# Fused chunk attention and gated FFN on one core: another order of casts, turns and loads in the first two blocks, and block 3's DMA turns behind four stores

## The chip, the core and the metric

The kernel runs on one NeuronCore of a Trainium2 chip. The time is device microseconds of one execution. Of the kernel before, three timed runs are known, 254.26, 256.61 and 257.28 us (median 256.61), and one profiled execution of 255.33 us, from which all readings of the trace come.

## What is computed

Attention over 4 batches, 8 heads, 768 tokens of 64 channels, in chunks of 32 tokens; a chunk sees 8 memory rows, 16 tokens to the left, itself and 8 tokens to the right. The result, with heads side by side as 512 channels, goes through a gated FFN with 1536 hidden channels.

```python
for c in range(nc):
    q_c = q[:, :, c_start:c_end]
    k_full = np.concatenate([mem_k, k_ctx], axis=2)
    v_full = np.concatenate([mem_v, v_ctx], axis=2)
    scores = scale * np.matmul(q_c, k_full.transpose(0, 1, 3, 2))
    a = softmax(scores)
    out[:, :, c_start:c_end] = np.matmul(a, v_full)
x = out.transpose(0, 2, 1, 3).reshape(B * S, H * D)
return np.maximum(x @ w_gate, 0.0) * (x @ w_val) @ w_out
```

## The kernel before

**Blocks.** The 3072 tokens are cut into 8 blocks n of 384 (two for each batch). A block's attention goes by four head pairs hp, and inside a pair by four windows of 96 queries against 128 keys. The schedule is written out by hand: each engine does its instructions in the order of the code.

**Keys and queries transposed ("turned").** Blocks 0 and 1 turn on TensorE: `turn_pe` (L182) multiplies the rows by a selection matrix (`sel`, built on GpSimd by `build_sel`, L397) for the keys and by `ident` for the queries, and `turn_copy` (L207) evicts both with VectorE. Block 0 reads f32 rows over the SP and ACT queues (`kst`, `qst`) and casts them to `lk`, `lq` pair by pair (`cast_k`, `cast_q`, L158 and L162, on whatever engine is named); block 1 gets its rows cast by GpSimd's own DMAs (L478 to L481). From block 2 on, `turn_dma` (L214) issues two DMA transposes on the SP queue, one for `kT`, one for `qT`, and `spread_q` (L222) copies `qT` into the block-diagonal `qbd` with two GpSimd copies.

**Attention of a pair.** Scores on TensorE (`step_s0` L232 in blocks 0 and 1, which multiplies a mask in first; `step_s` L249 later) into the one PSUM tile `sc_ps`; the exponential on ScalarE; values (`wide_v` L293, `step_v` L268), whose sums of the softmax come out of the same product; then Ln and Exp on ScalarE give the reciprocal, and VectorE multiplies (`wide_m`, `step_m`) into `xT`.

**FFN.** `ffn_unit` (L341) makes 128 hidden channels of a block: 4 matmuls for the gate, 4 for the value, Relu on ScalarE, the product on VectorE. `out_unit` (L349) makes 128 tokens of output: 12 matmuls, a copy to `o_sb` on ScalarE, a store on the SP queue. The pool of `o_sb` has three buffers, the pool of PSUM tiles for turns, fillers, FFN and output (`fps`) four.

**The order around the change.** `fill(k)` issues k matmuls on zeros, which nothing reads. Block 0's turns, scores and values run first, then FFN unit 0 and 1 of block 0, block 1's turns, scores and values with its units 0 and 1, then units 2 to 11 of both blocks in turn (L563). After those come six output units u = 0 to 5 for blocks 0 and 1 (L578), with the attention of block 2 strewn between by the table `FIRST`; the scores of block 2's first pair stand ahead of u = 0. From block 2 on (L590) the attention of block n + 1 is strewn into the FFN of block n: the scores of block 3's first pair come after the 16 matmuls of block 2's FFN units 0 and 1.

GpSimd's queue carries: constants, block 0's values, a cast, the first 256 columns of both weights, two casts, block 1's rows and values, the other weight columns, `wo`, memsets, then for each block from 2 on `loads(n)` (4 DMAs of keys, 4 of queries, 4 of values) and `spread_q(n)`; `loads(n + 1)` stands behind `spread_q(n)`. A GpSimd DMA takes one of eight semaphores in turn, and waits until the DMA that had it last has landed. The SP queue carries the memory rows of a block (L139, L133), its two transposes and the stores. Before the change, block 3's transposes stand ahead of the stores of u = 0 to 5.

Of the kernel before, what the change touches and what calls it, by code (L numbers as in the profile page):

```python
# [18 lines left out]
def kernel(  # L19
# [31 lines left out]
    NFC = DM // 128  # L51
# [106 lines left out]
    def cast_k(hp, eng):  # L158
        eng(lk[:, hp].rearrange("p j h d -> p h j d"),
            kst[:, 2 * hp:2 * hp + 2, :].rearrange("p h (j d) -> p h j d", j=J))  # L160

    def cast_q(hp, eng):  # L162
        eng(lq[:, hp].rearrange("p j h d -> p h j d"),
            qst[:, 2 * hp:2 * hp + 2, :].rearrange("p h (j d) -> p h j d", j=J))
# [17 lines left out]
    def turn_pe(n, hp):  # L182

        kps = fps.tile([128, NQ, 128], F32, tag="f", name="k_ps")
        qps = fps.tile([128, 512], F32, tag="f", name="q_ps")[:, 0:TB]
        turns[n, hp] = kps, qps
        sel = sels[n].rearrange("p i t -> p (i t)")
        for j in range(J):
            kj = kps.rearrange("p i m -> p (i m)").rearrange("p (r j) -> p j r", j=J)[:, j]
            if n == 0:  # L190
                nc.tensor.matmul(kj, lhsT=lk[:, hp, j].rearrange("p h d -> p (h d)"), rhs=sel[0:KR + 2],  # L191
                                 start=True, stop=True)
            else:
                for hh in range(2):
                    nc.tensor.matmul(kj[D * hh:D * hh + D], lhsT=rk[:, 2 * hp + hh, j], rhs=sel[0:KR + 2],  # L195
                                     start=True, stop=True)
        for j in range(J):
            qj = qps.rearrange("p (r j) -> p j r", j=J)[:, j]
            if n == 0:
                nc.tensor.matmul(qj, lhsT=lq[:, hp, j].rearrange("p h d -> p (h d)"), rhs=ident[:QR, :QR],  # L200
                                 start=True, stop=True)
            else:
                for hh in range(2):
                    nc.tensor.matmul(qj[D * hh:D * hh + D], lhsT=rq[:, 2 * hp + hh, j], rhs=ident[:QR, :QR],
                                     start=True, stop=True)

    def turn_copy(n, hp):  # L207
        kps, qps = turns.pop((n, hp))
        if n not in qTs:
            qTs[n] = turned.tile([128, HP, TB], F16, tag="qT", name="qT0")  # L210
        dve_copy(kT_of(n)[:, :, hp, :], kps)
        dve_copy(qTs[n][:, hp, :], qps)
# [19 lines left out]
    def step_s0(n, hp):  # L232

        kT, qT = kT_of(n), qTs[n]
        sc = sps.tile([128, 2, 512], F32, name="sc_ps")
        mq = bass.AP(tensor=maskq.tensor, offset=maskq.offset, ap=[maskq.ap[0], [0, NQ], [1, QB]])
        for hh in range(2):
            nc.tensor.matmul(sc[:, hh, 0:TB].rearrange("p (i m) -> p i m", m=QB), lhsT=maskk, rhs=mq,  # L238
                             start=True, stop=False)
        for i in range(NQ):  # L240
            for hh in range(2):
                s = slice(D * hh, D * hh + D)
                nc.tensor.matmul(sc[:, hh, QB * i:QB * i + QB], lhsT=kT[s, i, hp, :],  # L243
                                 rhs=qT[s, hp, QB * i:QB * i + QB], start=False, stop=(i == NQ - 1))
        ex = epool.tile([128, 2, NQ, QB], F16, tag="ex", name="ex0")
        nc.scalar.activation(ex.rearrange("p h i m -> p h (i m)"), sc[:, :, 0:TB], ACT.Exp, scale=SCALE)  # L246
        exs[n, hp] = ex
# [45 lines left out]
    def wide_v(n, hp):  # L293

        ex = exs.pop((n, hp))
        vw = vwins[n % 2]
        if hp % 2 == 0:
            banks = [X[:, a, 0:TB] for a in range(2)]
        else:
            banks = [fps.tile([128, 512], F32, tag="f", name=nm)[:, 0:TB] for nm in ("xo_ps", "xs_ps")]  # L300
        for a in (1, 0):
            for i in range(NQ):
                for hh in range(2):
                    nc.tensor.matmul(banks[a][D * hh:D * hh + D, QB * i:QB * i + QB],
                                     lhsT=vw[:, i, 2 * hp + hh, D * a:D * a + D],
                                     rhs=ex[:, hh, i, :], start=True, stop=True)
        ln = rpool.tile([128, TB], F32, name="lnw")
        nc.scalar.activation(ln, banks[1], ACT.Ln, scale=1.0 / 64.0)
        rinv = rpool.tile([128, TB], F32, name="rinvw")
        nc.scalar.activation(rinv, ln, ACT.Exp, scale=-1.0, bias=mln64)  # L310
        wides[n, hp] = banks[0], rinv

    def wide_m(n, hp):
        o, rinv = wides.pop((n, hp))
        nc.vector.tensor_tensor(out=x_of(n)[:, hp, :], in0=o, in1=rinv, op=ALU.mult)  # L315
# [12 lines left out]
    def ffn_mm(n, order):  # L328
        for f, x in order:
            ps, w, m = units[n][x]  # L330
            nc.tensor.matmul(ps, lhsT=w[:, f, 128 * m:128 * m + 128], rhs=xTs[n][:, f, :],  # L331
                             start=(f == 0), stop=(f == NFC - 1))
# [57 lines left out]
    def mem_rows(p):  # L390
        src = bass.AP(tensor=mem16.tensor, offset=mem16.offset, ap=[mem16.ap[0], [0, NQ], [D, H], [1, D]])
        dve_copy(vwins[p][0:NMEM, :, :, 0:D], src)

    dve_copy(mem16, mem32)
    mem_rows(0)

    def build_sel(p):  # L397

        s = sels[p]
        nc.gpsimd.memset(s, 0.0)  # L400
        first = -6 if p == 0 else 10
        parts = [(0, NQ, 2, 32)] if p == 0 else [(0, NQ, 2, 30), (0, NQ - 1, 30, 32)]
        for i0, i1, t0, t1 in parts:
            ap = s[:, i0:i1, t0:t1]
            nc.gpsimd.affine_select(out=ap, in_=ap, compare_op=ALU.not_equal, fill=1.0,
                                    base=-first - t0, pattern=[[-24, i1 - i0], [-1, t1 - t0]], channel_multiplier=1)
        ap = s[:, :, 0:2]
        nc.gpsimd.affine_select(out=ap, in_=ap, compare_op=ALU.not_equal, fill=1.0,
                                base=-KR, pattern=[[0, NQ], [-1, 2]], channel_multiplier=1)
# [21 lines left out]
    def fill(count, cols=512):  # L431
        ps = fps.tile([128, 512], F32, tag="f", name="idle")
        for i in range(count):
            nc.tensor.matmul(ps[:, 0:cols], lhsT=filler[:, 0:128], rhs=filler[:, 0:cols], start=True, stop=True)  # L434

    act_copy = nc.scalar.copy
    fill(10)
    cast_k(0, dve_copy)
    cast_q(0, act_copy)
    turn_pe(0, 0)  # L440
    turn_copy(0, 0)
    fill(2)
    cast_k(1, act_copy)
    cast_q(1, act_copy)
    turn_pe(0, 1)
    fill(2)
    step_s0(0, 0)
    turn_copy(0, 1)
    cast_k(2, dve_copy)
    cast_q(2, pool_copy)  # L450
    load_w(wg, moe_w_gate, 0, 256)
    load_w(wv, moe_w_val, 0, 256)
    cast_k(3, pool_copy)
    cast_q(3, pool_copy)
    fill(2)
    step_s0(0, 1)
    turn_pe(0, 2)
    fill(1)
    wide_v(0, 0)
    turn_copy(0, 2)  # L460
    wide_v(0, 1)
    wide_m(0, 0)
    fill(2)
    turn_pe(0, 3)
    fill(1)
    step_s0(0, 2)
    turn_copy(0, 3)
    wide_m(0, 1)
    mem_rows(1)
    fill(2)  # L470
    step_s0(0, 3)
    wide_v(0, 2)
    wide_m(0, 2)
    fill(2)


    flat = rk.rearrange("p h j d -> p h (j d)")
# [1 line left out]
    for h0 in (0, 4):  # L479
        pool_dma(flat[0:KR, h0:h0 + 4], k_rows(1, h0, 4))  # L480
        pool_dma(rq.rearrange("p h j d -> p h (j d)")[:, h0:h0 + 4], q_rows(1, h0, 4))  # L481
    build_sel(1)
    load_band(1, v, vwins)
    for c0, c1 in ((256, 768), (768, 1280), (1280, 1536)):
        load_w(wg, moe_w_gate, c0, c1)
# [5 lines left out]
    for a in range(0, NDC, 4):  # L491
        pool_dma(wo[:, a:a + 4, :], wo_src[:, a:a + 4, :])

    wide_v(0, 3)
    wide_m(0, 3)
    ffn_open(0, (0,))
    for f in range(3):
        ffn_mm(0, [(f, 0), (f, 1)])
    turn_pe(1, 0)
    ffn_mm(0, [(3, 0), (3, 1)])  # L500
    ffn_close(0)
    turn_copy(1, 0)
    ffn_unit(0, 1)
    turn_pe(1, 1)
    step_s0(1, 0)
    turn_copy(1, 1)
    fill(2)
    step_s0(1, 1)
    turn_pe(1, 2)
    fill(1)  # L510
    wide_v(1, 0)
    turn_copy(1, 2)
    wide_v(1, 1)
    wide_m(1, 0)
    fill(2)
    turn_pe(1, 3)
    fill(1)
    step_s0(1, 2)
    turn_copy(1, 3)
    wide_m(1, 1)  # L520
    fill(2)
    step_s0(1, 3)
    wide_v(1, 2)
    wide_m(1, 2)
    fill(2)
    wide_v(1, 3)
    wide_m(1, 3)
    ffn_open(1, (0,))
    for f in range(4):
        ffn_mm(1, [(f, 0), (f, 1)])  # L530
    ffn_close(1)
    ffn_unit(1, 1)
# [24 lines left out]
    turn_dma(2)  # L557
    spread_q(2, pool_copy)
    loads(3)
    turn_dma(3)  # L560
    spread_q(3, pool_copy)

    for m in range(2, NDC):  # L563
        ffn_unit(0, m)
# [5 lines left out]
    def pieces(n, what):  # L570
        for w, hp in what:
            STEP[w](n, hp)
# [5 lines left out]
    for u in range(6):  # L578
        pieces(2, FIRST.get(2 * u, ()))
        out_unit(u // 3, u % 3, lambda: pieces(2, FIRST.get(2 * u + 1, ())))  # L580

# [58 lines left out]
```

## Time and profile before

| | |
|---|---|
| timed runs | 254.26, 256.61, 257.28 us, median 256.61 |
| the profiled execution | 255.33 us, of which the span of its instructions is 253.6 us |
| TensorE busy with matmuls | 235.2 us, 93% of the span |
| ScalarE, GpSimd, VectorE busy | 141.0, 113.2 and 99.1 us |
| moved by DMA | 28.95 MB, 114 GB/s on average |
| granted TensorE clock, mean | 0.980 |

The busy times are averages over stages of different kinds: a start, in which rows come in and the first two blocks are turned and scored (to 39.5 us), FFN units alone (39.5 to 66.8 us), output units with block 2's attention (66.8 to 94.7 us), and six blocks of FFN with the next block's attention between (from 94.7 us). What an edit is worth is read in its own stage, and in what stands behind it.

### The profile page before, as it was taken

The numbers are of one execution on the slowest core, as the hardware profiler recorded it, in microseconds if no ns is written. First come the engines' busy times: TensorE is split into PE (matmuls) and PEld (weight loads), VectorE is DVE, ScalarE is ACT, GpSimd is POOL, SyncE is SP. The second block draws the span as 40 slices with busy tenths as digits, with TensorE's granted clock in tenths as the row PEclk, the third lists the DMA queues.
The fourth block names the chain that finished last, engine by engine and source line by source line (L and its number), as shares of the span: only waits on it lengthen the run. The fifth ranks groups of instructions, "written<-read, shape, count | busy, mean of one in ns | idle before, by whom it ended". The sixth has DMA issues, their size and how long they took to land.

```text
span 253.6 us, 4446 instructions
## 1 busy us (share of the span) xinstructions
PE 235.2 (93%) x1682; PEld 135.8 (54%) x1682; DVE 99.1 (39%) x181; ACT 141.0 (56%) x268; POOL 113.2 (45%) x143
## 2 busy tenths in 40 slices
PE   6798998999999088999999999999999999999993
PEld 2554545666554045664666456655665566546641
DVE  6653644444311021662156314640565055604410
ACT  2165374333483455984588448955796378723311
POOL 8999479921990595079208920892040000000000
PEclk9799999999999859999999999999999999999999
DMA  7999999999599899919971997199620300020012
GB/s 180 199 146 168 206 194 206 160 151 101 35 144 140 208 118 172 129 36 155 192 134 20 135 200 139 26 130 207 114 41 4 124 1 3 0 105 19 3 41 83
DMA packets 114111, 28.95 MB, mean 114 GB/s; under 512 B 101834, under 2 KB 111018, under 8 KB 114090
## 3 DMA queue, kind: packets, MB, share of 16 engines
q0 software_dynamic: 84896, 14.74, 72.7%
q1 hardware_dynamic: 28362, 13.14, 24.6%
q10 hardware_dynamic: 832, 0.79, 1.2%
q8 instruction: 13, 0.21, 0.3%
q14 instruction: 8, 0.07, 0.1%
HBM read 31.16 MB, written 6.29 MB: 148 GB/s over the span
## 4 chain that ended last, share of the span: by engine, by line
PE 85%; ACT 5%; DMA 4%; issue 2%; DVE 1%; SPq 1%; ACTq 0%
PE v_ps L331 24%; PE g_ps L331 24%; PE o_ps L354 23%; PE x_ps L273 3%; PE sc_ps L253 3%; DMA out_dram<-o_sb 3%; DMA mem<-in_mem_v_dram 2%; PE idle L434 1%; PE sc_ps L238 1%; ACT ex L246 1%; PE k_ps L191 1%; PE sc_ps L243 1%; PE k_ps L195 1%; ACT ex L260 1%; ACT ln L276 1%
## 5 line engine op out<-in xcount | busy, mean ns | idle before, releaser
L339 DVE TENSOR_TENSOR gv<-v_ps,gr 128x384 f16<-128x384 f32 x96 | 53.5, 558 | 99.3 <-ACT gr L338 73.5
L331 PE MATMUL g_ps<-xT,wg 128*128 128x384 f16 x384 | 80.1, 326 | 1.6 <-DVE xT L315 1.2
L331 PE MATMUL v_ps<-xT,wv 128*128 128x384 f16 x384 | 80.0, 326 | 0.2 <-ACT o_sb L357 0.2
L354 PE MATMUL o_ps<-wo,gv 128*128 128x512 f16 x288 | 66.2, 387 | 0.0
L338 ACT ACTIVATE gr<-g_ps 128x384 f16<-128x384 f32 x96 | 46.7, 487 | 31.5 <-DVE gv L339 21.8
L331 PEld LDWEIGHTS <-wg 128*128 128x128 f16 x384 | 37.2, 98 | 23.9 <-issue 1.1
L331 PEld LDWEIGHTS <-wv 128*128 128x128 f16 x384 | 36.4, 98 | 23.8 <-issue 1.8
L226 POOL COPY qbd<-qT 64x1536 f16<-64x1536 f16 x12 | 17.5, 1462 | 68.1 <-DMA qT<-q16n 67.7
L354 PEld LDWEIGHTS <-gv 128*128 128x128 f16 x288 | 28.5, 100 | 33.1 <-issue 2.5
L357 ACT COPY o_sb<-o_ps 128x512 f32<-128x512 f32 x24 | 14.1, 587 | 44.0 <-PE o_ps L354 36.3
L288 DVE TENSOR_TENSOR xT<-x_ps,rinv 64x384 f16<-64x384 f32 x48 | 26.4, 550 | 26.8 <-ACT rinv L281 26.5
L260 ACT ACTIVATE ex<-sc_ps,bias 128x256 f16<-128x256 f32 x72 | 28.6, 467 | 2.6 <-PE sc_ps L253 2.5
L128 POOL DMA_DIRECT2D vwin<-in_v_dram x32 | 29.5, 948 | 0.6 <-issue 0.4
L276 ACT ACTIVATE ln<-x_ps 64x768 f32<-64x768 f32 x24 | 19.4, 807 | 13.8 <-PE x_ps L273 13.7
L281 ACT ACTIVATE rinv<-ln,mln 64x768 f32<-64x768 f32 x24 | 22.2, 924 | 0.1
L128 POOL DMA_DIRECT2D k<-in_k_dram x24 | 21.5, 905 | 0.0
L273 PE MATMUL x_ps<-ex,vwin 128*128 128x96 f16 x192 | 12.5, 209 | 8.0 <-ACT ex L260 8.0
L149 POOL DMA_DIRECT2D q16n<-in_q_dram x24 | 18.6, 801 | 0.0
L273 PEld LDWEIGHTS <-vwin 128*128 128x128 f16 x192 | 11.1, 99 | 11.9 <-DVE xT L288 7.8
L434 PE MATMUL idle<-filler 128*128 128x512 f16 x34 | 12.7, 478 | 1.3 <-DVE filler L370 1.3
L246 ACT ACTIVATE ex<-sc_ps 128x768 f16<-128x768 f32 x8 | 6.5, 811 | 9.9 <-PE sc_ps L243 9.9
L253 PE MATMUL sc_ps<-qbd,kT 128*128 128x192 f16 x96 | 11.8, 246 | 0.0
(70 smaller groups left out, 107.5 us busy)
## 6 DMA issues: line engine op xcount, KB each, us to landing
out_dram<-o_sb SPq DMA_DIRECT2D x24, 256.0 KB
vwin<-in_v_dram POOLq DMA_DIRECT2D x24, 120.0 KB, 5.7
q16n<-in_q_dram POOLq DMA_DIRECT2D x24, 96.0 KB, 4.4
k<-in_k_dram POOLq DMA_DIRECT2D x18, 120.0 KB, 4.4
wo<-in_moe_w_out_dram POOLq DMA_DIRECT2D x3, 512.0 KB, 13.4
wg<-in_moe_w_gate_dram POOLq DMA_DIRECT2D x2, 512.0 KB, 8.9
wv<-in_moe_w_val_dram POOLq DMA_DIRECT2D x2, 512.0 KB, 10.7
kst<-in_k_dram SPq DMA_DIRECT2D x4, 224.0 KB
```

The source lines that it names most:

```text
L128: pool_dma(dsts[p][NMEM + m0:NMEM + m1, i, :, 0:D], src)
L149: pool_dma(q16s[n][:, i], src)
L253: nc.tensor.matmul(sc[:, i // 2, 192 * (i % 2):192 * (i % 2) + 192], lhsT=kT[:, i, hp, :], rhs=qb[:, i, hp].rearrange("p h m -> p (h m)"), ...
L260: nc.scalar.activation(dst, src, ACT.Exp, scale=SCALE, bias=bias[:, g:g + 1])
L273: nc.tensor.matmul(X[:, hh, QB * i:QB * i + QB], lhsT=vw[:, i, 2 * hp + hh, :], rhs=ex[:, i, hh, :], start=True, stop=True)
L276: nc.scalar.activation(ln, X[D:128, :, 0:TB], ACT.Ln, scale=1.0 / 64.0)
L281: nc.scalar.activation(rinv, lns.pop((n, hp)), ACT.Exp, scale=-1.0, bias=mln64[0:D, :])
L288: nc.vector.tensor_tensor(out=xT[D * hh:D * hh + D, hp, :], in0=X[0:D, hh, 0:TB], in1=rinv[:, hh, :], op=ALU.mult)
L331: nc.tensor.matmul(ps, lhsT=w[:, f, 128 * m:128 * m + 128], rhs=xTs[n][:, f, :], start=(f == 0), stop=(f == NFC - 1))
L338: nc.scalar.activation(gr, g_ps, ACT.Relu)
L339: nc.vector.tensor_tensor(out=gvs[n][:, m, :], in0=v_ps, in1=gr, op=ALU.mult)
L354: nc.tensor.matmul(o_ps, lhsT=gvs[n][:, m, 128 * t:128 * t + 128], rhs=wo[:, m, :], start=(m == 0), stop=(m == NDC - 1))
```

## The change

It does four things.

**Block 0.** The first `fill` has 16 matmuls where there were 10. The memory rows for the values (a cast and a copy on VectorE) move from ahead of the first key cast to behind the first pair's eviction. Pair 0 is scored before pair 1 is turned; pairs 2 and 3 are turned before the scores of pairs 1 and 2. The key cast of pair 2 goes from VectorE to ScalarE, and GpSimd does its three casts before its first two weight loads, with block 1's `sel` built ahead of the casts. In all, fillers after the first batch go from 14 to 10.

**Block 1.** Unit 0 of block 0's FFN is no longer split around `turn_pe(1, 0)`, and the turns stand further ahead of the scores; fillers go from 10 to 2.

**Block 3.** `turn_dma(3)` and `spread_q(3)` move from ahead of the FFN units into the loop of output units, behind u = 3.

```diff
-    dve_copy(mem16, mem32)
-    mem_rows(0)
...
-    fill(10)
+    fill(16)
     cast_k(0, dve_copy)
     cast_q(0, act_copy)
     turn_pe(0, 0)
     turn_copy(0, 0)
-    fill(2)
+    fill(3)
     cast_k(1, act_copy)
     cast_q(1, act_copy)
+    build_sel(1)
+    dve_copy(mem16, mem32)
+    mem_rows(0)
+    step_s0(0, 0)
     turn_pe(0, 1)
+    turn_copy(0, 1)
+    cast_k(2, act_copy)
+    cast_q(2, pool_copy)
+    cast_k(3, pool_copy)
+    cast_q(3, pool_copy)
+    fill(3)
+    step_s0(0, 1)
+    turn_pe(0, 2)
+    turn_copy(0, 2)
     fill(2)
-    step_s0(0, 0)
-    turn_copy(0, 1)
-    cast_k(2, dve_copy)
-    cast_q(2, pool_copy)
+    wide_v(0, 0)
+    turn_pe(0, 3)
+    step_s0(0, 2)
+    turn_copy(0, 3)
+    wide_m(0, 0)
+    mem_rows(1)
+    wide_v(0, 1)
+    fill(1)
+    step_s0(0, 3)
+    wide_m(0, 1)
+    fill(1)
+    wide_v(0, 2)
+    wide_m(0, 2)
+    wide_v(0, 3)
+    wide_m(0, 3)
     load_w(wg, moe_w_gate, 0, 256)
     load_w(wv, moe_w_val, 0, 256)
-    cast_k(3, pool_copy)
-    cast_q(3, pool_copy)
-    fill(2)
-    step_s0(0, 1)
-    turn_pe(0, 2)
-    fill(1)
-    wide_v(0, 0)
-    turn_copy(0, 2)
-    wide_v(0, 1)
-    wide_m(0, 0)
-    fill(2)
-    turn_pe(0, 3)
-    fill(1)
-    step_s0(0, 2)
-    turn_copy(0, 3)
-    wide_m(0, 1)
-    mem_rows(1)
-    fill(2)
-    step_s0(0, 3)
-    wide_v(0, 2)
-    wide_m(0, 2)
-    fill(2)
...
-    build_sel(1)
     load_band(1, v, vwins)
...
-    wide_v(0, 3)
-    wide_m(0, 3)
     ffn_open(0, (0,))
-    for f in range(3):
+    for f in range(NFC):
         ffn_mm(0, [(f, 0), (f, 1)])
     turn_pe(1, 0)
-    ffn_mm(0, [(3, 0), (3, 1)])
+    turn_copy(1, 0)
     ffn_close(0)
-    turn_copy(1, 0)
     ffn_unit(0, 1)
     turn_pe(1, 1)
+    turn_copy(1, 1)
     step_s0(1, 0)
-    turn_copy(1, 1)
-    fill(2)
+    turn_pe(1, 2)
+    turn_copy(1, 2)
     step_s0(1, 1)
-    turn_pe(1, 2)
-    fill(1)
     wide_v(1, 0)
-    turn_copy(1, 2)
-    wide_v(1, 1)
-    wide_m(1, 0)
-    fill(2)
     turn_pe(1, 3)
-    fill(1)
     step_s0(1, 2)
     turn_copy(1, 3)
+    wide_m(1, 0)
+    wide_v(1, 1)
+    fill(1)
+    step_s0(1, 3)
     wide_m(1, 1)
-    fill(2)
-    step_s0(1, 3)
+    fill(1)
     wide_v(1, 2)
     wide_m(1, 2)
-    fill(2)
     wide_v(1, 3)
     wide_m(1, 3)
...
     loads(3)
-    turn_dma(3)
-    spread_q(3, pool_copy)
...
     for u in range(6):
         pieces(2, FIRST.get(2 * u, ()))
         out_unit(u // 3, u % 3, lambda: pieces(2, FIRST.get(2 * u + 1, ())))
+        if u == 3:
+            turn_dma(3)
+            spread_q(3, pool_copy)
```

**On the SP queue**, between block 3's memory rows and block 4's (`k_101` is block 3's key tile, `L359` a store of an output unit), the difference is this piece:

```order
 L133 DMA vwin_103<-mem 8x8x64 x4
+L359 DMA out_dram<-o_sb 128x512 x4
 L216 DMA_TRANSPOSE kT<-k_101 128x16x128
 L219 DMA_TRANSPOSE qT<-q16n 128x16x96
-L359 DMA out_dram<-o_sb 128x512 x6
+L359 DMA out_dram<-o_sb 128x512 x2
 L139 DMA k_100<-mem 8x4x512
```

The stores of u = 0 to 3 now stand ahead of block 3's two transposes, those of u = 4 and 5 still behind them. On GpSimd nothing moves there: `spread_q(3)` still stands between `loads(3)` and `loads(4)`.

**On GpSimd**, from the last constant to the first rows of block 1 (`lq_117` and `lk_116` are block 0's cast rows, `lk_118` and `lq_119` those of block 1, `sel_95` block 1's selection matrix), before:

```order
L427 AFFINE_SELECT maskq<-maskq 128x96
L163 CAST lq_117<-qst 96x2x4x64
L152 DMA wg<-in_moe_w_gate_dram 128x4x256
L152 DMA wv<-in_moe_w_val_dram 128x4x256
L159 CAST lk_116<-kst 114x2x4x64
L163 CAST lq_117<-qst 96x2x4x64
L478 DMA lk_118<-in_mem_k_dram 2x8x256
L480 DMA lk_118<-in_k_dram 112x4x256
```

and in the changed kernel:

```order
L424 AFFINE_SELECT maskq<-maskq 128x96
L397 MEMSET sel_95 128x128
L402 AFFINE_SELECT sel_95<-sel_95 128x4x28
L402 AFFINE_SELECT sel_95<-sel_95 128x3x2
L405 AFFINE_SELECT sel_95<-sel_95 128x4x2
L163 CAST lq_117<-qst 96x2x4x64
L159 CAST lk_116<-kst 114x2x4x64
L163 CAST lq_117<-qst 96x2x4x64
L152 DMA wg<-in_moe_w_gate_dram 128x4x256
L152 DMA wv<-in_moe_w_val_dram 128x4x256
L477 DMA lk_118<-in_mem_k_dram 2x8x256
L479 DMA lk_118<-in_k_dram 112x4x256
```

The two weight loads fall behind the other two casts and the building of `sel_95`, and every DMA behind them on this queue keeps its place in the row.

**On VectorE**, at the first cast (`mem_105`, `mem_106` are the memory rows in f32 and f16, `vwin_102` block 0's values), the changed kernel has:

```order
L379 MEMSET vwin_103 24x8x32
L159 CAST lk_116<-kst 114x2x4x64
L211 CAST kT<-k_ps 128x4x128
L212 CAST qT_196<-q_ps 128x384
L443 CAST mem_106<-mem_105 8x512
L392 COPY vwin_102<-mem_106 8x32x64
```

Before, the two operations on the memory rows stood between the memset and the key cast.

More of the change, by code (lines that the diff above doesn't have):

```diff
@@ L528 @@
     ffn_open(1, (0,))
-    for f in range(4):
+    for f in range(NFC):
         ffn_mm(1, [(f, 0), (f, 1)])
```

## Prediction

> **What bounds the kernel now.** I read the slices of the page first, then the busy time by stages, then the timeline of the stages in which TensorE isn't full.
>
> ```profile
> PE   6798998999999088999999999999999999999993
> PEclk9799999999999859999999999999999999999999
> 66.80:82.30 15.50, 15.47 (x102) 8.12 (x99) 2.76 (x5) 8.71 (x17) 8.98 (x11) 1.00 1.79 129
> 82.30:89.60 7.30, 0.00 (x0) 0.06 (x1) 1.10 (x2) 3.56 (x7) 4.24 (x4) 0.84 0.80 184
> 89.60:94.70 5.10, 5.07 (x20) 2.25 (x21) 1.10 (x2) 2.19 (x3) 5.10 (x7) 0.56 1.51 135
> 100.00:122.20 22.20, 22.20 (x152) 12.97 (x150) 9.98 (x18) 15.12 (x29) 12.97 (x14) 1.00 1.26 112
> ```
>
> TensorE is full and at full clock from 100 us to the last output unit, so the end comes as much earlier as block 3's first scores (97.66 us) do. Two places ahead of them aren't full: the start, and 82.3 to 89.6 us, an empty stretch with 5 us at 0.56 of the clock behind it. The second has its cause in these rows, of SP, GpSimd, ScalarE and TensorE:
>
> ```profile
> 72.35 3.66 SPq L216 DMA_TRANSPOSE kT<-k  x1
> 76.24 2.75 SPq L219 DMA_TRANSPOSE qT<-q16n  x1
> 79.09 16.77 SPq L359 DMA_DIRECT2D out_dram<-o_sb  x6
> 85.31 2.98 POOL L226 COPY qbd<-qT 64x1536 f16<-64x1536 f16 x2 [9.53 <-DMA qT<-q16n]
> 85.96 0.59 ACT L357 COPY o_sb<-o_ps 128x512 f32<-128x512 f32 x1 [7.63 <-DMA out_dram<-o_sb]
> 89.63 0.80 PE L273 MATMUL x_ps<-ex,vwin 128*128 128x96 f16 x8 [7.35 <-ACT ex L260]
> 90.22 4.66 PE L354 MATMUL o_ps<-wo,gv 128*128 128x512 f16 x12
> 67.15 2.75 PE L354 MATMUL o_ps<-wo,gv 128*128 128x512 f16 x12
> 97.66 0.49 PE L253 MATMUL sc_ps<-qbd,kT 128*128 128x192 f16 x4
> ```
>
> SP stands in its transposes while the first copies wait to be stored; with three `o_sb` buffers full, u = 3's copy waits 7.63 us for a store to land, ScalarE's queue stands behind it, and TensorE waits 7.35 us for an exponential. Its next 12 matmuls take 4.66 us where the same 12 took 2.75: 1.9 us more.
>
> **The stores ahead of the transposes.** First without any other shift. Unit 3 runs here:
>
> ```profile
> 76.26 2.75 PE L354 MATMUL o_ps<-wo,gv 128*128 128x512 f16 x12
> 94.72 0.33 PE L331 MATMUL g_ps<-xT,wg 128*128 128x384 f16 x1
> ```
>
> It ends at 79.0. Its copy no longer waits: it starts at 79.05 instead of 85.96. From that copy's start to the values of pair 3 the trace has 89.63 - 85.96 = 3.67 us (copy, Ln, Exp, exponentials), so these values come at 82.7, 0.6 us after TensorE has done unit 4. Then 8 matmuls (0.34), unit 5 (2.6 at full clock), and 97.66 - 94.72 = 2.94 us to the end of the 16 FFN matmuls: TensorE reaches block 3's first scores at 88.6 and not 97.66, **9.1 us earlier**. That removes the wait and its half clock.
>
> What is late next are the transposes, which began at 72.35 and now begin behind the fourth store: copy done at 79.65, store issued by 80.1. From the start of a turn to the first `qbd` copy the six turns differ:
>
> ```profile
> 50.90 4.26 SPq L216 DMA_TRANSPOSE kT<-k  x1
> 62.72 2.98 POOL L226 COPY qbd<-qT 64x1536 f16<-64x1536 f16 x2 [10.35 <-DMA qT<-q16n]
> 100.71 2.83 SPq L216 DMA_TRANSPOSE kT<-k  x1
> 109.17 2.98 POOL L226 COPY qbd<-qT 64x1536 f16<-64x1536 f16 x2 [10.60 <-DMA qT<-q16n]
> 127.93 2.01 SPq L216 DMA_TRANSPOSE kT<-k  x1
> 134.30 2.98 POOL L226 COPY qbd<-qT 64x1536 f16<-64x1536 f16 x2 [12.04 <-DMA qT<-q16n]
> 72.22 3.56 POOL L128 DMA_DIRECT2D vwin<-in_v_dram  x4
> 94.89 3.68 POOL L128 DMA_DIRECT2D vwin<-in_v_dram  x4
> 118.66 3.60 POOL L128 DMA_DIRECT2D vwin<-in_v_dram  x4
> ```
>
> 11.8 us for block 2, 13.0 for block 3 (72.35 to 85.31), 8.5 for block 4, 6.4 for block 5. Block 3's starts with the issue of its value loads, block 4's 2.1 us after the end of that issue (98.57), block 5's 5.7 us after it (122.26). In the new place block 3's value loads are all issued by 75.8, or 77.3 with the delay of the next part, and the turn starts 4 to 5 us later, so I take 6.4 and add 0.4 for the store just ahead on the same queue: 6.8; bounds 6.4 and 13.0. With the 2.98 us of the copies, `qbd` is ready 9.8 us after the turn starts: at 89.9, **1.3 us after TensorE gets there**.
>
> The page "DMA: Bandwidth & Descriptors" of the Trainium skill (Queues, rings and completion order) states that each DMA engine round-robins between its queues packet by packet; the four durations agree with that.
>
> **GpSimd's casts ahead of its weight loads.** These are the rows at that place, and the one at which the weight queue lets GpSimd go:
>
> ```profile
> 9.42 0.79 POOL L152 DMA_DIRECT2D wg<-in_moe_w_gate_dram  x1
> 10.20 0.76 POOL L152 DMA_DIRECT2D wv<-in_moe_w_val_dram  x1
> 11.29 0.86 POOL L159 CAST lk<-kst 114x512 f16<-114x512 f32 x1 [0.32 <-DMA kst<-in_k_dram]
> 12.65 0.60 POOL L478 DMA_DIRECT2D lk<-in_mem_k_dram  x1
> 16.96 3.96 POOL L128 DMA_DIRECT2D vwin<-in_v_dram  x4
> 33.41 0.74 POOL L492 DMA_DIRECT2D wo<-in_moe_w_out_dram  x1 [1.28 <-DMA wg<-in_moe_w_gate_dram]
> 66.82 0.49 PE L253 MATMUL sc_ps<-qbd,kT 128*128 128x192 f16 x4
> ```
>
> The key cast waits for rows until 11.29 in any order, so the casts end at 12.65 as before, and the weight loads are issued then, 3.2 us later than 9.42. Behind them block 1's rows are issued 0.79 + 0.76 = 1.55 us later; block 1's values, with `sel_95` already built, 0.65 us later. The DMA engines are the bound of this stream, for GpSimd waits at 33.41 for a weight load to land. So the whole stream is late by something between 0.65 (what the issues lose at last) and 3.2 (if no idle time of the engines makes up for any); I take **1.5**, the shift of block 1's rows. It passes on undiminished: the last `wo` load, the memsets, the loads of block 2, its turn at 50.90, and its `qbd`, ready at 62.72 + 2.98 = 65.70 before, at 67.2 now.
>
> **The start of blocks 0 and 1 gets shorter, for nothing.**
>
> ```profile
> 7.69 0.61 PE L191 MATMUL k_ps<-sel,lk 114*128 114x128 f16 x4 [2.10 <-DVE lk L159]
> 8.70:12.20 3.50, 3.50 (x16) 2.04 (x16) 2.33 (x5) 0.06 (x1) 3.18 (x6) 0.51 1.73 196
> 1.27 4.32 PE L434 MATMUL idle<-filler 128*128 128x512 f16 x10 [1.27 <-DVE filler L370]
> 6.62 0.68 DVE L392 COPY vwin<-mem 8x2048 f16<-8x2048 f16 x1
> 39.20 0.32 PE L331 MATMUL g_ps<-xT,wg 128*128 128x384 f16 x1 [0.54 <-DVE xT L315]
> ```
>
> Without the memory rows ahead of it the key cast can start about 1 us earlier, and 16 fillers end near 6.9 (ten in 4.32 us, six at the 0.22 us of 2.6 / 12); the first turn moves from 7.69 to about 6.9: 0.8 us. The 2.1 us gap goes, and with it the stretch at half clock that follows it (3.5 us at 0.51 in the row above, so 3.4 us at half): 1.7 us. Eight fillers fewer in block 1: 1.7 us. Sum 4.2, so the last of unit 0's inputs, 39.20 now, comes near 35; a wait for block 1's later rows is in this only as its lower bound, 0. If the new order of turns hides more, it is 5.5. TensorE would be through with the FFN units, which run without a gap, at 66.82 - 4.2 = 62.6.
>
> There it meets block 2's first scores, which stand ahead of unit 0 on TensorE and need the `qbd` of 67.2. It was 1.1 us from waiting there (65.70 against 66.82); it now waits **4.6 us**, and starts 0.4 us later than before. Whatever the start saves above nothing is lost here; this holds for any saving from 0 to 5.5.
>
> **The clock after that wait.** The 7.35 us gap cost 1.9 us of half clock, the 2.10 us gap 3.4 us of it. I take 1.9 for 4.6 us; bounds 0 (no drop) and 2.2 (0.56 on average over 5.1 us is 4.5 us at half clock, and half of that is lost).
>
> The page "TensorE: Matmul & The Clock Gate" of the Trainium skill (Part 1, What's actually happening) puts the drop at an idle window of about 3.4 us; by it the 4.6 us would do it, and half a window is an estimate of 1.7 us. The 2.10 us gap, shorter than such a window, dropped the clock too: the trace is stricter.
>
> **Sum.** Block 2's scores 0.4 later, half clock 1.9: everything behind shifts by 2.3. TensorE reaches block 3's scores at 88.6 + 2.3 = 90.9; the turn starts at 82.4 and `qbd` is ready at 82.4 + 9.8 = 92.2. So 92.2 against 97.66: **5.5 us gained**. The loads of block 4, behind `spread_q(3)`, start at 92.2 instead of 88.3. From the end of block 2's copies (65.70) to that of block 3's (88.29), at the slowest turn, went 22.6 us, so block 4's `qbd` is ready by 114.8; its scores come 25.7 us after block 3's,
>
> ```profile
> 123.33 0.49 PE L253 MATMUL sc_ps<-qbd,kT 128*128 128x192 f16 x4
> ```
>
> at 117.9. That cover, 3 us, holds. The profiled execution would take 255.33 - 5.5 = 249.8. The mean of the four known executions is 255.87, so I add 0.5: **250.3 us**.
>
> **Rivals.**
> 1. *The first wait costs no clock* (its gap falls across the windows in which the clock is set, or the start saves little). Then block 3's scores come at 80.1 + 0.4 + 9.8 = 90.3, 7.4 gained: 248.4. For it: of the 7.3 us from 82.3 some 5 passed at full clock (a mean of 0.84 is 2.3 us at half). Against it: both gaps seen dropped the clock in the end. With the stream late by only 0.65 it is 247.4.
> 2. *A turn like block 4's* (8.5 us), with a second drop of the clock after a wait of 3 us: scores at 82.4 + 8.5 + 3.0 = 93.9, and 1.8 of half clock: 2.0 gained, 253.8, no change that shows. For it: a store's data and 2.3 us of shift in the loads lie nearer than in block 5's turn.
> 3. *Slower: the turn is slow by itself.* If it still takes 13.0 us, `qbd` comes at 82.4 + 13.0 + 3.0 = 98.4; TensorE waits 7.5 us and loses 1.9 of clock: 2.6 lost, 258.4. From 10.5 us on (with the drop) nothing is gained. For it: two of six turns were that slow. Against it: both had value loads beside them.
>
> **How the numbers follow.** The forecast gets 0.54, rival 1 0.17, rival 2 0.20, rival 3 0.09. The forecast's own range, by its bounds, is 248.3 to 252.3; 247.0 to 254.3 takes in rivals 1 and 2 and leaves out rival 3 and the tails. About 2% of 256.61 can be told from no change: below 251.5 counts as faster, above 261.7 as slower. Below 251.5 lie four fifths of the forecast and rival 1: 0.61. Slower needs rival 3 with further losses (block 4's turn late, the stream at its upper bound): 0.04. The rest is 0.35.
>
> **What would show it.** Right: ScalarE's wait of 7.63 us for `out_dram` is gone; a new gap on TensorE of 3 to 6 us before the first L253 at about 67 us, ended by GpSimd's `qbd`, with half clock behind; first weight loads issued near 12.7; block 3's first scores near 92, again behind `qbd`, full from there on. Wrong: block 2's `qbd` ready before TensorE, a turn of block 3 over 9 us, or gaps after 100 us.

## The result, and the profile after

The changed kernel takes **248.66 us** in the median of four runs (248.13 to 249.34). Before took 256.42 in the median of four runs. The ratio is 0.971, with a 95% interval of 0.965 to 0.978: faster, by 2.2% to 3.5%. The profiled execution took 248.73 us, with a span of 247.0; before's took 255.33 with 253.6. So 6.6 us of the span are to be explained, and the forecast for this execution was 249.8, 5.5 us less than before.

The slices of the page after the change, TensorE's busy share and its granted clock:

```profile
PE   7998989999499979999999999999999999999993
PEclk9999999999779999999999999999999999999998
```

The hole that stood in slices 14 and 15 is gone. A new one stands in slice 11 (62 to 68 us), with a lower clock on it and on the slice behind it. From slice 16 on TensorE is full, as before. The busy time by stages gives the clock of the new hole (the columns are the stretch, its length, the busy time of TensorE's matmuls, its weight loads, VectorE, ScalarE and GpSimd, then the clock, the DMA share and GB/s):

```profile
60.00:66.00 6.00, 2.66 (x17) 1.75 (x16) 1.12 (x3) 0.98 (x2) 3.69 (x3) 0.86 0.37 68
66.00:72.00 6.00, 6.00 (x24) 2.43 (x23) 0.00 (x0) 1.94 (x5) 6.00 (x9) 0.57 1.67 106
```

0.86 over 6 us is 1.7 us at half clock, and 0.57 is 5.2 us more: 6.8 us, from about 64.4 to 71.2. The timeline of TensorE shows what made it:

```profile
34.16 0.32 PE L331 MATMUL g_ps<-xT,wg 128*128 128x384 f16 x1 [0.54 <-DVE xT L315]
...
61.13 0.81 PE L331 MATMUL v_ps<-xT,wv 128*128 128x384 f16 x4
65.28 0.80 PE L253 MATMUL sc_ps<-qbd,kT 128*128 128x192 f16 x4 [3.34 <-POOL qbd L226]
65.88 5.33 PE L354 MATMUL o_ps<-wo,gv 128*128 128x512 f16 x12
...
84.07 0.50 PE L273 MATMUL x_ps<-ex,vwin 128*128 128x96 f16 x8 [0.44 <-ACT ex L260]
...
91.08 0.49 PE L253 MATMUL sc_ps<-qbd,kT 128*128 128x192 f16 x4 [0.97 <-POOL qbd L226]
```

The row at 34.16 stood at 39.20 before: the start of blocks 0 and 1 is 5.0 us shorter. TensorE is through with the FFN units at 61.94, waits 3.34 us for block 2's `qbd`, and does the next 12 matmuls in 5.33 us instead of 2.75. Of the wait of 7.35 us for an exponential, 0.44 is left (84.07). Block 3's first scores come at 91.08, 6.58 us earlier than before, and the span is shorter by the same 6.6 us.

GpSimd and the SP queue, from the timeline:

```profile
35.02 0.74 POOL L490 DMA_DIRECT2D wo<-in_moe_w_out_dram  x1 [1.26 <-DMA wg<-in_moe_w_gate_dram]
...
50.62 3.61 POOL L128 DMA_DIRECT2D vwin<-in_v_dram  x4 [0.57 <-PE v_ps L331]
62.26 2.98 POOL L226 COPY qbd<-qT 64x1536 f16<-64x1536 f16 x2 [8.02 <-DMA qT<-q16n]
...
71.75 3.60 POOL L128 DMA_DIRECT2D vwin<-in_v_dram  x4
88.04 2.98 POOL L226 COPY qbd<-qT 64x1536 f16<-64x1536 f16 x2 [12.69 <-DMA qT<-q16n]
```

```profile
52.81 4.42 SPq L216 DMA_TRANSPOSE kT<-k  x1
...
71.85 9.49 SPq L359 DMA_DIRECT2D out_dram<-o_sb  x4
81.58 2.03 SPq L216 DMA_TRANSPOSE kT<-k  x1
83.83 1.72 SPq L219 DMA_TRANSPOSE qT<-q16n  x1
```

The weight stream lets GpSimd go at 35.02 instead of 33.41, 1.6 us late. Yet block 2's `qbd` copies begin at 62.26, *earlier* than before's 62.72: the turn that began at 52.81 took 9.45 us, where the one that began at 50.90 took 11.8. Four stores now pass ahead of block 3's transposes, which take 6.46 us from 81.58 to the copies at 88.04. The row for the copy to `o_sb` in the list of instruction groups, before and after, shows the removed wait (its last column is ScalarE's idle time ahead of the copy, and what ended it):

```profile
L357 ACT COPY o_sb<-o_ps 128x512 f32<-128x512 f32 x24 | 14.1, 587 | 44.0 <-PE o_ps L354 36.3 <-DMA out_dram<-o_sb 7.6
L357 ACT COPY o_sb<-o_ps 128x512 f32<-128x512 f32 x24 | 14.1, 587 | 37.7 <-PE o_ps L354 37.7
```

### The profile page after: what moved, and what is told of

It reads as the page before. It is cut to its first block, busy times and chain, and to the rows that moved or that the text cites. A ratio compares the mean times of both kernels' runs of the same rounds, so it can differ in the third digit from the quotient of the medians.

```text
span 247.0 us, 4433 instructions
## 1 busy us (share of the span) xinstructions
PE 233.5 (95%) x1676; PEld 135.4 (55%) x1676; DVE 99.7 (40%) x180; ACT 141.5 (57%) x269; POOL 112.6 (46%) x143
## 4 chain that ended last, share of the span: by engine, by line
PE 71%; POOL 9%; DMA 9%; issue 7%; ACT 2%; DVE 0%; SPq 0%; POOLq 0%
PE g_ps L331 23%; PE v_ps L331 23%; PE o_ps L354 19%; DMA kst<-in_k_dram 4%; PE x_ps L273 3%; PE sc_ps L253 3%; DMA vwin<-in_v_dram 3%; POOL vwin L128 2%; POOL qbd L226 2%; DMA qT<-q16n 2%; POOL k L128 1%; POOL q16n L149 1%; POOL lq L480 1%; POOL lk L479 1%; ACT lnw L308 1%
## 5 line engine op out<-in xcount | busy, mean ns | idle before, releaser
L354 PE MATMUL o_ps<-wo,gv 128*128 128x512 f16 x288 | 66.9, 390 | 0.0
L276 ACT ACTIVATE ln<-x_ps 64x768 f32<-64x768 f32 x24 | 19.4, 807 | 13.5 <-PE x_ps L273 13.4
L273 PE MATMUL x_ps<-ex,vwin 128*128 128x96 f16 x192 | 12.3, 207 | 1.1 <-ACT ex L260 1.1
L253 PEld LDWEIGHTS <-kT 128*128 128x128 f16 x96 | 8.7, 99 | 7.8 <-issue 4.8
L431 PE MATMUL idle<-filler 128*128 128x512 f16 x28 | 10.0, 491 | 1.3 <-DVE filler L370 1.3
```

Source lines behind the costliest of these rows:

```text
L253: nc.tensor.matmul(sc[:, i // 2, 192 * (i % 2):192 * (i % 2) + 192], lhsT=kT[:, i, hp, :], rhs=qb[:, i, hp].rearrange("p h m -> p (h m)"), ...
L273: nc.tensor.matmul(X[:, hh, QB * i:QB * i + QB], lhsT=vw[:, i, 2 * hp + hh, :], rhs=ex[:, i, hh, :], start=True, stop=True)
L354: nc.tensor.matmul(o_ps, lhsT=gvs[n][:, m, 128 * t:128 * t + 128], rhs=wo[:, m, :], start=(m == 0), stop=(m == NDC - 1))
```

## The experiments

Four questions were open: which of the change's parts brings the gain, what the new wait costs, why the stream's delay didn't arrive, and what sets block 3's first scores now. Runs of before on the same chip as each batch: median 255.65 for the first four kernels, 255.25 for the next four, 255.61 for the last four.

### Which part brings the gain

**The stores alone.** Before, with block 3's two calls moved and nothing else:

```diff
     loads(3)
-    turn_dma(3)
-    spread_q(3, pool_copy)
...
         out_unit(u // 3, u % 3, lambda: pieces(2, FIRST.get(2 * u + 1, ())))
+        if u == 3:
+            turn_dma(3)
+            spread_q(3, pool_copy)
```

> The kernel before with only block 3's transposes moved behind u = 3; the start as it was. Theory (the stores' order brings the gain, and the new start is lost in the wait for block 2's qbd): block 2's first scores stay at 66.8 us with no wait and no half clock, the turn starts at 80.1, takes 6.5 + 3.0, block 3's first scores come at 89.6 against 97.7 before and 91.1 in the change: 247.2 us, 1.5 us faster than the change. Rival (the new start brings its 5 us too, and the stores the rest): 1.6 us under before, about 253.7 us.

247.92 us, ratio 0.969 (0.963 to 0.975). The timelines of TensorE and GpSimd in this kernel:

```profile
67.84 0.49 PE L253 MATMUL sc_ps<-qbd,kT 128*128 128x192 f16 x4
...
91.11 0.49 PE L253 MATMUL sc_ps<-qbd,kT 128*128 128x192 f16 x4 [1.34 <-POOL qbd L226]
```

```profile
64.81 2.98 POOL L226 COPY qbd<-qT 64x1536 f16<-64x1536 f16 x2 [10.99 <-DMA qT<-q16n]
...
88.08 2.99 POOL L226 COPY qbd<-qT 64x1536 f16<-64x1536 f16 x2 [10.14 <-DMA qT<-q16n]
```

Block 2's first scores come 2.6 us later than in the change, without a wait and without half clock, and block 3's `qbd` copies begin at the same time (88.08 and 88.04). The theory held in what brings the gain. The 1.5 us under the change that it also expected are not there: the profiled span is 247.0 us in both, and the ratios overlap.

**The new start alone.** The change, with block 3's two calls back ahead of the FFN units (the same diff, reversed):

> The changed kernel with block 3's transposes put back ahead of the stores. Theory: TensorE ends the FFN units 5 us earlier and waits 3 us for block 2's qbd; the half clock after it runs into the wait for a store, which ends 0.5 us earlier than before because block 2's qbd does: 254.8 us (254 to 255.5), within 1% of before. Rival (the start's saving counts): 250.3 us.

255.64 us in ten runs, ratio 1.001 (0.997 to 1.005). TensorE's timeline:

```profile
65.98 0.49 PE L253 MATMUL sc_ps<-qbd,kT 128*128 128x192 f16 x4 [3.87 <-POOL qbd L226]
66.31 4.44 PE L354 MATMUL o_ps<-wo,gv 128*128 128x512 f16 x12
...
89.69 0.80 PE L273 MATMUL x_ps<-ex,vwin 128*128 128x96 f16 x8 [6.57 <-ACT ex L260]
...
97.88 0.49 PE L253 MATMUL sc_ps<-qbd,kT 128*128 128x192 f16 x4
```

The saved 5 us become a wait of 3.87 and a slow stretch, and the old wait is back with 6.57 us. The theory held, with the time 0.1 us above its range. So the whole gain is the order of the SP queue; the new start is worth nothing that can be measured, alone or beside it.

### What the new wait costs

**The wait filled.** The change, with 15 matmuls on zeros ahead of block 2's first scores, which keep TensorE busy through the wait:

```diff
+    fill(15)
     for u in range(6):
```

> The changed kernel with 15 fillers (3.3 us at full clock) ahead of block 2's first scores. Theory (the half clock after the wait costs its full 2.9 us, since block 3's turn stands behind u = 3's store): the scores stay at 65.3, no half clock, the turn starts at 78.7 instead of 81.6, block 3's first scores at 88.2: 245.8 us. Rival (the clock's loss is absorbed, for the stores and loads on the DMA engines set the turn): 248.7 us.

247.41 us, ratio 0.968 (0.962 to 0.973); mean clock 1.0 in all four executions. TensorE's timeline and the SP queue's:

```profile
61.86 3.40 PE L431 MATMUL idle<-filler 128*128 128x512 f16 x15
65.96 0.49 PE L253 MATMUL sc_ps<-qbd,kT 128*128 128x192 f16 x4 [0.70 <-POOL qbd L226]
66.29 2.75 PE L354 MATMUL o_ps<-wo,gv 128*128 128x512 f16 x12
...
89.54 0.49 PE L253 MATMUL sc_ps<-qbd,kT 128*128 128x192 f16 x4 [1.66 <-POOL qbd L226]
```

```profile
79.36 3.07 SPq L216 DMA_TRANSPOSE kT<-k  x1
```

The half clock is gone and the 12 matmuls are back at 2.75. But only 1.5 us of the 2.9 arrive at block 3's scores: block 2's scores were 0.7 us later in this execution, the turn began 2.2 us earlier (79.36) but took 7.1 us, and 1.66 us of waiting for `qbd` are left. That lies between the theory and the rival, and it is the trace that shows it: the ratio overlaps with the change's.

### Why the stream's delay did not arrive

**The weights ahead of the casts again.** The change, with the two first weight loads back between GpSimd's casts:

```diff
     cast_q(2, pool_copy)
+    load_w(wg, moe_w_gate, 0, 256)
+    load_w(wv, moe_w_val, 0, 256)
     cast_k(3, pool_copy)
...
-    load_w(wg, moe_w_gate, 0, 256)
-    load_w(wv, moe_w_val, 0, 256)
```

> The changed kernel with GpSimd's two weight loads between its first and second cast, as they stood before. Theory (the weight stream sets block 2's qbd): loads of block 2 issued 1.5 us earlier, at 41.7; its first scores at 63.8 instead of 65.3, the wait 1.9 us; 247.2 us if the clock drops all the same, 245 if it doesn't. Rival (the length of block 2's turn sets it, not the stream): no move beyond 0.5 us, 248.7 us.

247.87 us, ratio 0.971 (0.965 to 0.976). Block 2's turn begins 2.1 us earlier than in the change, at 50.73, and block 2's scores come 0.6 us *later*. SP, then GpSimd:

```profile
50.73 4.04 SPq L216 DMA_TRANSPOSE kT<-k  x1
```

```profile
62.88 2.98 POOL L226 COPY qbd<-qT 64x1536 f16<-64x1536 f16 x2 [10.29 <-DMA qT<-q16n]
```

The turn took 12.15 us: the earlier start is eaten whole by a longer turn. The rival held.

**Block 2's loads ahead of `wo`.** The change, with `loads(2)`, and the two short memsets it needs, ahead of the three loads of `wo`:

```diff
+    loads(2)
     for a in range(0, NDC, 4):
         pool_dma(wo[:, a:a + 4, :], wo_src[:, a:a + 4, :])
...
-    loads(2)
     turn_dma(2)
```

> The changed kernel with block 2's loads ahead of the three loads of wo on GpSimd, and the long memsets behind them. Theory (the new start's 5 us come through once block 2's qbd is there in time, and wo has time until 62 us): block 2's first scores at 61.9 without a wait and without half clock, block 3's turn at 75.2, its first scores at 84.8 against 91.1 in the change: 242.4 us. Rival (block 2's turn is as slow beside the wo loads as beside its own value loads, or slower, and wo comes late): its qbd at 64 or later, half clock again, 246 to 249 us.

250.87 us, ratio 0.983 (0.978 to 0.988): worse than the change. The theory fell; the rival had the mechanism, and the time is above even its range. SP and GpSimd:

```profile
45.82 4.35 SPq L216 DMA_TRANSPOSE kT<-k  x1
50.40 5.15 SPq L219 DMA_TRANSPOSE qT<-q16n  x1
```

```profile
47.18 2.29 POOL L500 DMA_DIRECT2D wo<-in_moe_w_out_dram  x3
65.25 2.98 POOL L226 COPY qbd<-qT 64x1536 f16<-64x1536 f16 x2 [9.30 <-DMA qT<-q16n]
```

The turn began 7 us earlier and ended 3 us later: 19.4 us beside the three `wo` loads, whose median time to landing is 13.1 us.

**The value loads first.** The change, with block 2's value loads ahead of its key and query loads, so that they have landed when the turn begins (the last is issued at 45.8 us and lands 5.6 us later, at about 51.4):

```diff
-    loads(2)
+    load_band(2, v, vwins)
+    load_v_mem(2)
+    load_band(2, k, k16s)
+    load_k_mem(2)
+    load_q_tokens(2)
```

> The changed kernel with block 2's value loads ahead of its key and query loads. Theory (a turn is long because value loads are in flight beside it, and turn and loads together take a fixed time): the turn starts 3 us later, near 55.5, and takes 6.4 to 8 us instead of 9.5 to 12.9; qbd ready at 65 to 66.5, 248.7 us within 1. Rival (the length has another cause): 9.5 us or more from the later start, qbd at 68 or later, 251 us or more.

248.99 us in the median of five, ratio 0.975 (0.971 to 0.980); the profiled execution was the fastest of them, 246.0. SP, GpSimd and TensorE:

```profile
54.91 3.14 SPq L216 DMA_TRANSPOSE kT<-k  x1
```

```profile
62.03 2.98 POOL L226 COPY qbd<-qT 64x1536 f16<-64x1536 f16 x2 [8.59 <-DMA qT<-q16n]
```

```profile
65.06 0.49 PE L253 MATMUL sc_ps<-qbd,kT 128*128 128x192 f16 x4 [3.35 <-POOL qbd L226]
65.39 2.75 PE L354 MATMUL o_ps<-wo,gv 128*128 128x512 f16 x12
```

Now the turn takes 7.1 us, but it begins 2.1 us later, and `qbd` is ready 0.2 us earlier than in the change. The theory held: the length of the turn follows the loads beside it, and moving them gains nothing. The rows of TensorE are a surprise: a wait of 3.35 us, as long as the change's 3.34, and no half clock behind it. The other four executions of this kernel had a mean clock of 0.983 to 0.990 and took 248.9 to 249.2 us; no trace shows where in them the clock was low.

### What sets block 3's first scores

**The turn behind three stores.** The change, with `if u == 2:` for `if u == 3:`.

> The changed kernel with block 3's turn behind u = 2 instead of u = 3: three stores ahead are enough for three buffers. Theory: the turn starts near 79.1, 2.5 us earlier, meets the last value loads (landed at 80.0) and takes 7.5; qbd near 89.6, before TensorE is there at 90.1, so the last wait of 1.0 us goes: 247.8 us. Rival (the value loads stretch the turn beyond 8.5, or the fourth copy waits for a store again): no gain or a loss, 248.7 to 251 us.

247.55 us, ratio 0.969 (0.964 to 0.975). The transposes begin at 80.04, the copies at 86.94, and TensorE finds `qbd` ready; the theory held, though block 2's scores came 1.1 us later in this execution. The ratio overlaps with the change's, so the trace shows the lost wait and the time does not:

```profile
90.82 0.49 PE L253 MATMUL sc_ps<-qbd,kT 128*128 128x192 f16 x4
```

**Both moves** (loads ahead of `wo`, turn behind three stores):

> f1 and f2 together. Theory: block 2's first scores at 61.9, block 3's turn at 72.6 and its first scores when TensorE gets there, at 83.8: 241.4 us. Rival: the value loads of block 3 land only at 75, so the turn behind three stores is stretched and gains nothing over f1, 242.4 us or more.

250.16 us, ratio 0.979 (0.975 to 0.984). The third store takes the last wait away here too, but block 2's turn again takes 20.1 us beside `wo`, so the theory fell with it. The rival's reason wasn't there either: block 3's turn took 6.9 us.

**The old start with the turn behind three stores**, that is before with only block 3's two calls moved, to `u == 2`:

> The kernel before, with only block 3's transposes and copies moved, behind the third store instead of the fourth. Theory (the turn's start sets block 3's qbd): the 1.34 us of wait that stood there behind the fourth store goes, 246.6 us. Rival (the turn gets longer by what it starts earlier, since the value loads are beside it): 247.9 us as behind the fourth store, with the wait of 1 to 1.5 us still there.

**246.10 us** in six runs (244.98 to 247.16), ratio 0.964 (0.960 to 0.968). The order of the start is before's. SP, GpSimd and TensorE:

```profile
77.57 3.67 SPq L216 DMA_TRANSPOSE kT<-k  x1
```

```profile
85.32 2.98 POOL L226 COPY qbd<-qT 64x1536 f16<-64x1536 f16 x2 [9.02 <-DMA qT<-q16n]
```

```profile
66.59 0.49 PE L253 MATMUL sc_ps<-qbd,kT 128*128 128x192 f16 x4
...
88.36 0.49 PE L253 MATMUL sc_ps<-qbd,kT 128*128 128x192 f16 x4
```

No wait at either place, and the copies end (88.30) just as TensorE arrives. The theory held. Of the 2.75 us between this and the stores alone, 1.25 are block 2's scores, which came that much later in that execution, and 1.34 the wait. The two ratios overlap, so it is the profile that tells these apart and not the time.

**Fill and three stores together**, on the change:

> The change with both small edits that helped alone: 15 fillers ahead of block 2's first scores, and block 3's turn behind the third store. Theory (TensorE sets the end: its clock loss of 2.9 us behind block 2's wait and its last wait of 1 us both go, and nothing takes their place): 245.2 us, block 3's first scores at 88 to 88.5 us. Rival (GpSimd's chain from block 2's qbd copies over block 3's loads and turn to its qbd sets block 3's scores, not before about 89.5): 246.5 to 247.4 us, and a wait of 1 to 2 us behind qbd at block 3's first scores.

246.24 us, ratio 0.964 (0.960 to 0.968): the same as the old start without these 15 fillers. Block 3's scores come at 89.39 behind 0.89 us of waiting; the time lies nearer to the rival's.

**Work in place of the wait.** The change, with the turn behind three stores, and output unit 0 ahead of block 2's first scores:

```diff
-    FIRST = {0: [("s", 0)], 2: [("v", 0), ("e", 0)], 3: [("s", 1), ("m", 0)], 5: [("v", 1), ("e", 1)],
-             6: [("s", 2), ("m", 1)], 8: [("v", 2), ("e", 2), ("s", 3)], 9: [("m", 2)], 10: [("v", 3), ("e", 3)],
+    FIRST = {2: [("s", 0)], 4: [("v", 0), ("e", 0), ("s", 1)], 5: [("m", 0)],
+             6: [("v", 1), ("e", 1), ("s", 2)], 7: [("m", 1)], 8: [("v", 2), ("e", 2), ("s", 3)], 9: [("m", 2)], 10: [("v", 3), ("e", 3)],
```

> The change, with output unit 0 ahead of block 2's first scores (real work in place of the wait; the steps of pairs 0 and 1 follow closer on each other) and block 3's turn behind the third store. TensorE would reach block 3's first scores near 84.5 us, 5.5 us earlier than in the change. Theory (TensorE sets the end): block 3's scores at 84.5 to 85.5, 242 to 243 us. Rival (GpSimd's chain to block 3's qbd sets it): scores at 88.5 to 90 behind a wait of 4 to 5 us for qbd that may bring half clock with it, 246 to 248.5 us: the wait has only moved from block 2 to block 3.

247.86 us, ratio 0.970 (0.966 to 0.974): the rival held, with a wait 1 us shorter than it said. TensorE and GpSimd:

```profile
62.56 2.75 PE L354 MATMUL o_ps<-wo,gv 128*128 128x512 f16 x12
65.62 0.49 PE L253 MATMUL sc_ps<-qbd,kT 128*128 128x192 f16 x4 [0.30 <-POOL qbd L226]
...
88.67 0.80 PE L253 MATMUL sc_ps<-qbd,kT 128*128 128x192 f16 x4 [3.05 <-POOL qbd L226]
```

```profile
85.63 2.98 POOL L226 COPY qbd<-qT 64x1536 f16<-64x1536 f16 x2 [9.98 <-DMA vwin<-mem]
```

The wait for block 2 is gone, and a wait of 3.05 us with half clock stands at block 3. With block 2's value loads first as well:

> As with output unit 0 ahead of block 2's first scores and the turn behind the third store, and block 2's value loads ahead of its key and query loads as well. Theory (TensorE sets the end): the same 242 to 243 us. Rival (GpSimd's chain sets it): block 3's scores at 88 to 89 behind a wait of 3.5 to 4.5 us, 245 to 248 us.

246.92 us, ratio 0.967 (0.964 to 0.971), block 3's scores at 89.21 behind 3.07 us of waiting, at full clock in the profiled execution. The rival held again, 0.2 us past its range at the scores and 0.4 us short of it at the wait.

### All of them beside each other

Times of one profiled execution each, in us; a turn runs from the start of its first transpose to the first `qbd` copy.

| kernel | block 2's turn | length | wait at its scores | block 3's turn | length | block 3's scores | wait | span |
|---|---|---|---|---|---|---|---|---|
| before | 50.90–62.72 | 11.8 | 0 | 72.35–85.31 | 13.0 | 97.66 | 0 | 253.6 |
| the change | 52.81–62.26 | 9.5 | 3.34 | 81.58–88.04 | 6.5 | 91.08 | 0.97 | 247.0 |
| stores alone | 51.95–64.81 | 12.9 | 0 | 81.24–88.08 | 6.8 | 91.11 | 1.34 | 247.0 |
| start alone | 52.64–62.95 | 10.3 | 3.87 | 72.36–85.37 | 13.0 | 97.88 | 0 | 253.8 |
| weights first | 50.73–62.88 | 12.2 | 3.88 | 82.23–88.74 | 6.5 | 91.78 | 1.02 | 247.7 |
| wait filled | 52.00–62.93 | 10.9 | 0.70 | 79.36–86.50 | 7.1 | 89.54 | 1.66 | 245.5 |
| loads ahead of `wo` | 45.82–65.25 | 19.4 | 5.66 | 83.66–90.10 | 6.4 | 93.14 | 0.95 | 249.0 |
| three stores | 53.13–63.33 | 10.2 | 4.05 | 80.04–86.94 | 6.9 | 90.82 | 0 | 246.7 |
| values first | 54.91–62.03 | 7.1 | 3.35 | 78.46–85.30 | 6.8 | 88.34 | 1.35 | 244.3 |
| loads ahead, three | 45.90–65.96 | 20.1 | 5.95 | 82.04–88.96 | 6.9 | 92.82 | 0 | 248.7 |
| filled, three | 52.51–63.54 | 11.0 | 1.44 | 77.56–86.35 | 8.8 | 89.39 | 0.89 | 245.3 |
| old start, three | 50.91–63.20 | 12.3 | 0 | 77.57–85.32 | 7.8 | 88.36 | 0 | 244.3 |
| unit 0 ahead | 53.48–62.59 | 9.1 | 0.30 | 73.41–85.63 | 12.2 | 88.67 | 3.05 | 246.7 |
| unit 0, values first | 56.17–63.10 | 6.9 | 1.21 | 73.93–86.17 | 12.2 | 89.21 | 3.07 | 245.1 |

Three things are read off it. The span ends 155.9 to 156.0 us after block 3's first scores in thirteen of the fourteen, and 158.0 in the one that has half clock behind them: what comes later takes equally long, that stretch of clock apart. Block 2's copies begin between 62.0 and 64.8 wherever its turn begins, from 50.7 to 56.2; only `wo` beside it makes them later. And from block 2's copies to block 3's it is never less than 22.1 us: block 3's loads stand behind block 2's copies on GpSimd, and the turn behind these loads gets longer when it starts sooner. So block 3's scores come no earlier than about 88.3 in any order of the start or of the output units profiled here. The old start with the turn behind three stores is at that floor.

The floor is that of the profiled executions. The fastest timed executions of the two kernels with the lowest times have spans of 243.3 and 243.4 us, which with the same 155.9 us behind them would put the scores near 87.5. And no run moves block 3's loads within GpSimd's queue, so it is not shown whether that order or the transfers themselves set the 22.1 us.

## Why the prediction was right, and where not

The direction, the cause and the range held. That the time came within 1.7 us of the 250.3 owes something to luck, for two terms of the sum were wrong in opposite directions. Its terms, against the profiled execution of the change:

| step | forecast | measured |
|---|---|---|
| TensorE is through with the FFN units | 62.6 | 61.94 |
| the weight stream is late by | 1.5 | 1.61 |
| block 2's turn | 11.8 (unchanged) | 9.45 |
| block 2's first scores | 67.2 | 65.28 |
| wait ahead of them | 4.6 | 3.34 |
| clock lost behind it | 1.9 (at most 2.2) | 2.9 |
| TensorE reaches block 3's scores | 90.9 | 90.11 |
| block 3's turn: start, length | 82.4, 6.8 | 81.58, 6.46 |
| block 3's first scores | 92.2, wait 1.3 | 91.08, wait 0.97 |
| gained | 5.5 | 6.6 |

- **Stores ahead of transposes: right.** The 7.63 us wait for `out_dram` is gone, and the turn that starts behind its value loads is as short as block 5's was. The table bears out the bounds that were drawn from the earlier turns. Block 3's took 12.2 to 13.0 us where it starts while the value loads are being issued, 7.8 to 8.8 about 1 us behind them, 6.4 to 7.1 from about 3 us behind them on. Rivals 2 and 3 needed 8.5 and 13.0 us.
- **"It passes on undiminished": wrong.** The stream was late by 1.6, as forecast, but the turn of block 2 took the delay up. The step took 11.8 us to be the turn's own length, when it was the length of a turn that overlaps the last value loads; block 2's `qbd` came at 65.24 us and not at 67.2. Weights first (earlier start, longer turn), values first (7.1 us without them beside it) and loads ahead of `wo` (19.4 us with more beside it) show that the work beside it sets its length. The prediction had used just this rule for block 3, and not for block 2.
- **The half clock: a size that was off.** 1.9 us was read off one wait, and the upper bound off the same stretch. The loss was 2.9: 6.8 us at half, of which 5.9 lie behind the resumption. Behind the wait of 7.35 us the stretch was as long, but 2.4 us of it lay inside the wait, where they cost nothing. The size isn't fixed either: two of the change's four executions had a mean clock of 0.993, where the profiled one had 0.983, and took 0.2 and 0.6 us less. The forecast was 1.0 too little, against 1.9 us too much for the late `qbd`: together 0.9 of the 1.1 us by which the forecast of block 3's scores was late. The first error hid part of the second.
- **"Whatever the start saves above nothing is lost here": right**, with 5.0 saved instead of 4.2. Of the parts, the half clock in the start is gone, and the first turn came at 7.22 us and not at 6.9; the four fillers fewer in block 0, about 0.9 us by the price of the others, were left out of the sum. The start alone is at 1.001 (0.997 to 1.005).
- **The sum.** The time, 248.66, lies nearest to rival 1's 248.4, but rival 1 said that the first wait would cost no clock, and it cost 2.9 us. The forecast's mechanism is the one that ran in the profiled execution, with a smaller wait and a larger loss. The 0.5 us added for the mean of the known runs were not needed: the median is 0.07 below the profiled execution.

## What to carry to other kernels

A queue that carries both transposes and stores is an order of priorities: put what returns a buffer ahead of what is needed only later, and ask how long the moved transfer will take *in its new place*, among the loads that will then be beside it. Before shortening a stage, look for the transfer that the next stage waits for: here 5 us of shorter start bought only a wait, and the old start did no worse. When one wait is gone, look for the shortest time that the chain behind it has taken (here 22.1 us from one block's copies to the next's): none of the orders tried on TensorE got below that.

## What the runs showed of the hardware

**A wait of the same length may or may not cost the clock.** In the profiled executions, waits of 2.10 (before), 2.34 (old start, three), 3.05, 3.34, 3.87, 3.88, 4.05, 5.66, 5.95, 6.57 and 7.35 us came with half clock, and waits of 1.73 (stores alone, at the start), 3.07 and 3.35 us did not. The stretch at half clock had one of two lengths. It was 3.4 us in the three cases where it began after TensorE had resumed (behind 2.10, 2.34 and 3.87), and 6.8 us in the eight where it began inside the wait. The values-first kernel took 246.0 us at a mean clock of 1.0, and 248.9 to 249.2 us at 0.983 to 0.990. The page "TensorE: Matmul & The Clock Gate" of the Trainium skill (Part 1, What's actually happening) says that the activity window of about 3.4 us runs freely, so that the moment of a change depends on where in the window the work begins. The two lengths, one and two such windows, and the two outcomes at nearly the same wait agree with that. The drops behind 2.10, 2.34, 3.05 and 3.34 us don't agree with the idle window of that length after which the Trainium skill puts the drop.

**A pair of DMA transposes of the same 384 tokens took from 6.4 to 20.1 us**, from the start of the first to the copy that waits for them, by what GpSimd's loads were moving beside it: 7.1 us with the value loads landed before, 9.5 beside them, 19.4 beside the three loads of `wo` (block 2's turn in values first, the change, and loads ahead of `wo`). With the same two instructions and the same sizes each time, a duration taken from one place of the program said little of another.
